# Gated attention and state-space mix on one core: parameters transposed by the DMA, maxima read from PSUM, dummy products, and a reordered prologue

## Chip, cores and metric

The kernel runs on one core of a Trainium2 chip. The metric is the time of one execution in microseconds (us), measured on the device. Three executions of the kernel before took 514.63, 514.94 and 518.87 us; the median is 514.94. A further execution, recorded by the hardware profiler, took 513.35 us. All durations below come from that recording.

The engines are named as in the profile: PE (TensorE, the matrix engine; PEld is its loading of weights), DVE (VectorE), ACT (ScalarE), POOL (GpSimd) and SP (SyncE, which here only issues DMA transfers). SBUF is the core's working memory and PSUM the memory into which PE writes.

## The reference

The input x has 2048 tokens of 448 channels (bfloat16). Two branches are computed from it and mixed by a gate:

- `g = sigmoid(sum(x * gate_w))`, one number per token.
- Branch a is attention with 16 query heads of width 28 that share one key head and one value head: `softmax(q k^T / sqrt(28)) v`, then a product with `wo`.
- Branch b is a long convolution of every channel along the tokens. Its kernel is generated from parameters: `K[d, l] = Re(sum_n C[d,n] * exp(l * dt[d] * A[d,n]) * dt[d] * B[d,n])`, with 256 complex terms per channel and 2048 positions. `u * Dskip` is added. A, B and C come as real and imaginary arrays of 448 x 256: six arrays, named A_im, A_re, B_re, B_im, C_re and C_im below, in the order in which the kernel numbers them (0 to 5).
- The result is `g * a + (1 - g) * b`.

## The kernel before

Attention is split into 1024 score tiles of 128 keys by 512 queries. Sets of three and two tiles alternate, 410 sets in all. For each set PE writes the scores to PSUM (`qk`, L1172 or L1181), ACT turns them into exponentials in SBUF (L1204), and PE multiplies these with the values (`pv`, L1218). The scores have two forms. The row-packed one (L1172) uses the 29 rows of one head; the full one (L1181) uses 128 rows and a copy of the queries, `qM`, in which other heads are zero. `qM` is filled by a DMA that POOL issues (L138). A set uses the row-packed form for sets 0 to 5, and from set 44 to 410 where it has three tiles.

Meanwhile DVE builds the powers of exp(dt A) for blocks of channels (`masters`, L845 to L865, and `tables`, L883 to L929; `BLOCKS` says which channels form a block), PE turns them into the convolution kernel (`kgen`, L949), which goes through DRAM (KP_scratch) and comes back as Toeplitz tiles `T`, and PE convolves (L1010). The input of the convolution, `U`, is x in another order: DMA loads put x into `O` (queue slots u0 and u1, eight transfers each), POOL copies it to `U` (L565, four copies for each half), and a DMA named du moves one half across partitions. The gaps of `U` are zeroed by four memsets beforehand (`consts`, on DVE before the change).

The order of the work is made by a planner (`Prog.schedule`) when the program is built. Every operation has an engine, a planned duration, a priority and lists of what it reads and writes. The planner runs a model of the engines and writes one list of instructions for each, in which the engine then works strictly in order; waits are put in where data or buffers require them. `pg.after[i] = j` tells the planner to place operation i after j and puts no wait into the program. Some constants steer the model: HEAD (how much later an operation may be ready and still be preferred for its longer path to the first exponential), FETCH, AHEAD, PORT. `tail` is the longest path from an operation to the first exponential, the planner's `goal`.

The prologue is the stretch up to that first exponential, and a short one behind it:

- SP issues the loads in one queue, in this order: the four quarters of x with wk and A_im between them, wq, wv, the other five parameters, zeros for Wo (zW), Dskip, the store xs1, a pad, xs2 and xs3, then u, wo and more. xs1 to xs3 store the transposed x of three quarters of the tokens to DRAM, from where they are read again later. The buffer of the last quarter is overwritten by the exponentials of the third set.
- PE transposes x (L606); ACT and DVE copy it out of PSUM (L615, L617); PE projects the keys (L620), with the key weight that L532 has copied into its padded form `Wk`. The keys stay in PSUM until ACT writes them to `kT` (L629).
- The largest absolute key of each quarter is needed for a bound on the scores that takes the place of the softmax's running maximum. DVE takes it from `kT` for the first three quarters (L633) and from PSUM for the fourth (L626).
- The maxima scale a mask into the weight `Wb` (L653, L654). For the first group of heads the queries are projected (L808), their maximum is taken (L814), the product with `Wb` is added (L817) and the result is cast to `qT` (L820). Then the first scores (L1172) and the first exponential can run. L534 and L536 copy the query weights to padded form.
- Each parameter arrives as 112 partitions by 1024 elements and is transposed by eight PE products into PSUM (`trans`, L738). DVE multiplies it (L749) with dt or with an earlier product. Between these, POOL reduces the angle (L752, L753) and makes the cosine term from a sine (L773, L774), and ACT computes sines, decays and squares (L758, L766, L769).
- The gate: ACT's exponential (L667), DVE's L669 to L671, a PE product (L686), a DVE copy `acc`, a second PE product (L696) and a copy to `omq` (L701).

## Time and profile before

| | us |
|---|---|
| runs | 514.63, 514.94, 518.87 (median 514.94) |
| the profiled execution | 513.35 |
| its span, first to last instruction | 511.6 |
| first exponential starts | 23.24 |
| last exponential ends | 500.97 |
| ACT busy | 485.7 |
| of that the 410 exponentials | 467.2 |

A group line of the profile names the source line, the engine, the operation and its tiles, then the count, busy time, mean ns of one, the idle time of the engine ahead of them and what ended it. A line of a timeline gives the start, the duration, the engine, source line, operation, tiles and count; several instructions that follow each other are one line; brackets hold the idle time before it and what released it. A line of the waits gives total us, count and longest. The rows of the page cut into 40 slices hold tenths: PEclk is the clock granted to PE. A row of a windows table names the stretch, its length, then for PE, PEld, DVE, ACT and POOL the busy time with the count of instructions, then the granted clock, the busy share of the DMA engines and GB/s.

Loads reach SBUF in the order of SP's queue. From the trace: the quarters of x land at 4.01, 6.72, 8.76 and 10.91, wk at 4.19, A_im at 7.68, wq at 12.29, A_re at 13.23, B_re, B_im, C_re and C_im at 14.06, 14.89, 15.98 and 16.95, zW at 18.25, the stores xs1, xs2 and xs3 at 19.39, 21.53 and 22.63, and u's first half at 25.75 us.

### The profile page before, as it was taken

What the parts mean: (1) busy time and instruction counts of PE and PEld (TensorE: products, weight loads), DVE (VectorE), ACT (ScalarE), POOL (GpSimd) and SP (SyncE); (2) the same over time, 40 slices, a digit from 0 to 9 for tenths busy, and PEclk for the clock granted to TensorE, in tenths of its full rate; (3) what the DMA queues carried; (4) which work ended last, traced back from release to release, by engine and by line L of the source; (5) the groups of instructions that cost most, each with busy time, mean ns of one, the idle gap of its engine ahead of it and who ended that gap; (6) DMA issues with size and microseconds to landing.
All of it is one profiled execution on the core that took longest, in us unless ns stands there. A gap on an engine that the chain in (4) does not pass through costs nothing.

```text
span 511.6 us, 18576 instructions
## 1 busy us (share of the span) xinstructions
PE 431.2 (84%) x8249; PEld 196.9 (38%) x8355; DVE 455.5 (89%) x823; ACT 485.7 (95%) x436; POOL 169.3 (33%) x297
## 2 busy tenths in 40 slices
PE   6679777788888899888887898998888888999895
PEld 5433113243333333443433443443443434444452
DVE  6888999999999999999999999999999999712434
ACT  5789999999999999999999999999999999999991
POOL 7541503451132151424243334305234343341000
PEclk9859999799999999999999999999999999999999
DMA  8912496799979889799989899899997998999992
GB/s 237 288 27 70 36 60 169 209 310 339 346 220 279 284 250 369 245 305 312 368 275 342 305 305 349 254 352 351 328 363 257 366 351 259 372 279 369 361 359 49
DMA packets 113425, 140.27 MB, mean 274 GB/s; under 512 B 45497, under 2 KB 52058, under 8 KB 113346
## 3 DMA queue, kind: packets, MB, share of 16 engines
q1 hardware_dynamic: 103600, 129.77, 79.3%
q0 software_dynamic: 8704, 9.25, 6.9%
q8 instruction: 65, 1.06, 0.9%
q10 hardware_dynamic: 1042, 0.07, 0.1%
q14 instruction: 14, 0.11, 0.1%
HBM read 128.39 MB, written 5.22 MB: 261 GB/s over the span
## 4 chain that ended last, share of the span: by engine, by line
DVE 56%; ACT 32%; PE 8%; issue 1%; POOL 0%; another core or an unknown queue 0%; POOLq 0%
ACT expT L1204 32%; DVE tab L902 8%; DVE tab L914 5%; DVE tab L913 5%; DVE tab L912 4%; DVE tab L911 4%; DVE tab L924 3%; DVE msq L845 3%; DVE tmp L920 3%; DVE mbf L865 2%; DVE seedz L849 2%; DVE seedz L847 2%; DVE cst L1020 2%; PE psS L1181 2%; DVE qT L814 1%
## 5 line engine op out<-in xcount | busy, mean ns | idle before, releaser
L1204 ACT ACTIVATE expT<-psS 128x1536 bf16<-128x1536 f32 (+1 forms) x410 | 467.2, 1352 | 8.1 <-PE psS L1172 5.5
L1181 PE MATMUL psS<-qM,kT 128*128 128x512 bf16 (+1 forms) x381 | 116.2, 374 | 33.5 <-ACT expT L1204 20.3
L1218 PE MATMUL psB<-expT,vaug 128*32 128x512 bf16 (+1 forms) x1088 | 103.5, 380 | 3.4 <-DVE acc L1079 2.8
L1172 PE MATMUL psS<-qT,kT 29*128 29x512 bf16 (+1 forms) x603 | 75.7, 377 | 26.4 <-ACT expT L1204 20.1
L138 POOL DMA_DIRECT2D KP_scratch<-kstg x112 | 61.4, 556 | 63.2 <-DVE kstg L964 41.5
L902 DVE TENSOR_TENSOR tab<-tab,mbf 128x512 bf16<-128x512 bf16 (+3 forms) x56 | 65.5, 1170 | 0.0
L1218 PEld LDWEIGHTS psB<-expT,vaug 128*32 128x32 bf16 x1088 | 26.8, 93 | 83.5 <-issue 76.9
L1181 PEld LDWEIGHTS psS<-qM,kT 128*128 128x128 bf16 x485 | 31.2, 98 | 61.7 <-ACT expT L1204 44.2
L138 POOL DMA_DIRECT2D rdenB<-R_scratch x56 | 28.9, 522 | 67.7 <-DMA R_scratch<-denT 48.7
L1010 PE MATMUL psS<-T,U 128*20 128x128 bf16 (+7 forms) x1792 | 45.3, 220 | 1.3 <-issue 0.9
L138 POOL DMA_DIRECT2D qM<-qT x64 | 33.1, 525 | 30.6 <-DVE qT L820 20.2
L914 DVE TENSOR_TENSOR tab<-tab 128x128 bf16<-128x128 bf16 (+4 forms) x70 | 42.7, 611 | 0.0
L913 DVE TENSOR_TENSOR tab<-tab 128x128 bf16<-128x128 bf16 (+4 forms) x70 | 41.9, 599 | 0.1
L1172 PEld LDWEIGHTS psS<-qT,kT 29*128 29x128 bf16 x603 | 18.7, 91 | 58.2 <-ACT expT L1204 45.0
L1010 PEld LDWEIGHTS psS<-T,U 128*18 128x18 bf16 (+7 forms) x1792 | 30.9, 94 | 18.6 <-issue 13.1
L138 POOL DMA_DIRECT2D R_scratch<-denT x14 | 8.9, 638 | 72.7 <-DVE denT L1071 40.2
L912 DVE TENSOR_TENSOR tab<-tab,mbf 128x4096 bf16<-128x4096 bf16 x14 | 32.0, 2288 | 0.1
L924 DVE TENSOR_TENSOR tab<-tab,tmp 128x4096 bf16<-128x4096 bf16 x14 | 32.0, 2284 | 0.1
L911 DVE TENSOR_TENSOR tab<-tab,mbf 128x4096 bf16<-128x4096 bf16 x14 | 32.0, 2287 | 0.0
L949 PE MATMUL psX<-tab 128*32 128x64 bf16 x1280 | 29.8, 242 | 0.3 <-DVE tab L929 0.2
L949 PEld LDWEIGHTS psX<-tab 128*32 128x32 bf16 x1280 | 23.8, 117 | 10.9 <-issue 6.5
L845 DVE TENSOR_TENSOR msq<-seedz 128x256 f32<-128x256 f32 (+2 forms) x50 | 26.3, 525 | 0.2
(165 smaller groups left out, 531.1 us busy)
## 6 DMA issues: line engine op xcount, KB each, us to landing
T<-KP_scratch SPq DMA_DIRECT2D x176, 512.0 KB, 8.5
U<-KP_scratch SPq DMA_DIRECT2D x48, 512.0 KB, 9.1
rdenB<-R_scratch POOLq DMA_DIRECT2D x56, 64.0 KB, 5.6
qM<-qT POOLq DMA_DIRECT2D x64, 32.0 KB, 5.3
tab<-in_A_x_dram SPq DMA_DIRECT2D x4, 448.0 KB, 5.6
O<-in_A_x_dram SPq DMA_DIRECT2D x16, 112.0 KB, 2.7
O<-cst SPq DMA_DIRECT2D x1, 1792.0 KB, 27.9
KP_scratch<-kstg POOLq DMA_DIRECT2D x112, 16.0 KB, 4.5
```

What stands on the lines that cost most here:

```text
L138: return [e.dma_start(o, i, **kw) for o, i in pairs]
L902: vo(lambda e, dst=dst, src=src, mri=mri: e.tensor_tensor(dst, src, mri, ALU.mult), 4 * n, done + mk(lv), [kr, ki, tk])
L911: vo(lambda e, src=src, mi=mi, tv=tv: e.tensor_tensor(tv, src, mi, ALU.mult), 2 * n, done + mk(lv), [tk])
L912: vo(lambda e, dst=dst, src=src, mr=mr: e.tensor_tensor(dst, src, mr, ALU.mult), 2 * n, done + mk(lv), [kr, ki, ("gap", s)])
L913: vo(lambda e, dc=dc, tc=tc: e.tensor_tensor(dc[0], dc[0], tc[1], ALU.subtract), n, [tk, kr], [kr])
L914: vo(lambda e, dc=dc, tc=tc: e.tensor_tensor(dc[1], dc[1], tc[0], ALU.add), n, [tk, ki], [ki])
L949: r = e.matmul(G.v(32 * g, 32, 256 * q + 64 * k, [[1, 64]]), tab.v(0, P, so, [[4, 32]]), tab.v(0, P, fo, [[mo - fo, 2], [4, 32]]), start=( ...
L1010: r = e.matmul(ps.v(32 * j, 32 - 2 * n, 128 * k, [[1, 128]]), self.U.v(0, P, (4 * gi + j) * 32 + 2 * n, [[1, 32 - 2 * n]]), tbuf.v(0, P, t ...
L1172: r = e.matmul(self.psS.v(0, P, 512 * b + o, [[1, n]]), kT.v(32 * h, DH + 1, 128 * kt, [[1, 128]]), qT.v(32 * h, DH + 1, 512 * (i % 2) + q ...
L1181: r = e.matmul(self.psS.v(0, P, 512 * b + o, [[1, n]]), kT.v(0, P, 128 * kt, [[1, 128]]), self.qM.v(0, P, (i % 2) * XQ + 512 * h + qo, [[1 ...
L1204: pg.op("act", lambda e: e.activation(expT.v(0, P, 512 * es[0], spread(es, n)), self.psS.v(0, P, 512 * bs[0], spread(bs, n)), AF.Exp, scal ...
L1218: r = e.matmul(self.psB.v(32 * h, 32, qo, [[1, n]]), vaug.v(0, P, 32 * kt, [[1, 32]]), expT.v(0, P, 512 * ring[t] + o, [[1, n]]), start=(k ...
```

## The change

- Five of the six parameters (`FLIP`, all but A_re) are loaded by a transposing DMA in the place of the plain load, in the layout that the products need. Their 40 PE products go; DVE's products read them from SBUF. A_re keeps its PE transposes.
- The maxima of all four key quarters are read from PSUM (L654 of the changed kernel), and ACT's copy of a quarter to `kT` waits for its maximum.
- PE gets 13 products of 128 x 512 whose result nobody reads: four ahead of the first transpose of x, nine behind the last key projection.
- The four memsets of U move from DVE to POOL, where they stand behind the reduction of the angle. `qM` is zeroed in eight pieces rather than two. The copy that pads `Wk` moves to POOL. POOL first runs one TENSOR_SCALAR and one TENSOR_TENSOR on a single element.
- POOL's product for the cosine term (L810 of the changed kernel) is placed behind the cast of the first queries, by planner order alone.
- Two intermediate products move from `O` to `mbf`, so that the second half of u no longer waits for them. As a result all eight copies to U stand in one row on POOL.
- The planner's choice before the first exponential is rewritten: among the operations whose start is not later than the earliest one's by more than HEAD (now 0.6) of its duration, it takes the one with the longest path to the goal. FETCH goes from 6200 to 5900, AHEAD from 3000 to 2000, and some durations and priorities change (kgen 1.3 to 1.45, yt 1.45 to 1.55, outp 1.75 to 1.65).
- BLOCKS goes from 2, 2, 3, 3, 4 to 2, 3, 3, 3, 3 chunks. Row-packed scores begin at set 24.
- The lists that follow: SP now issues the Dskip and wo loads behind all of u; on PE the gate's two products stand ahead of the scores of the fifth and the sixth set (before: later); on ACT the third exponential follows behind four of the five L769 operations (L805 of the changed kernel) where it followed behind one.

```diff
+FLIP = (0, 2, 3, 4, 5)
-BLOCKS = ((0, 2), (2, 2), (4, 3), (7, 3), (10, 4))
+BLOCKS = ((0, 2), (2, 3), (5, 3), (8, 3), (11, 3))
...
         def fn(e):
+            if flip:
+                return [e.dma_start_transpose(o, i) for o, i in pairs]
             return [e.dma_start(o, i, **kw) for o, i in pairs]
...
-                        if early is None or r < early[0][0] and (r + self.HEAD < early[0][0] or tail[i] >= early[1]) or r <= early[2] + self.HEAD and tail[i] > early[1]:
-                            early = ((r, o.pr, i), tail[i], min(r, early[2]) if early else r)
-                        early = (early[0], early[1], min(r, early[2]))
+                        early.append((r, o.pr, i))
                         continue
...
+                if early:
+                    key = min(early)
+                    while True:
+                        later = [k for k in early if tail[k[2]] > tail[key[2]] and k[0] <= key[0] + self.HEAD * ops[key[2]].ns]
+                        if not later:
+                            break
+                        key = max(later, key=lambda k: tail[k[2]])
+                    if best is None or key < best[0]:
+                        best = (key, e, key[2])
...
+        def warm(e, n, b):
+            t, o = self.bank(b)
+            for _ in range(n):
+                r = e.matmul(t.v(0, P, o, [[1, 512]]), V(self.ident, 0, P), self.ident.v(0, P, 0, [[0, 4], [1, P]]),
+                             start=True, stop=True, tile_position=(0, 0), skip_group_check=True)
+            return r
...
+        for _ in range(4):
+            self.warm(1, 3, 430)
+        tiny = V(sm, 14, 1)
+        pm(tiny, 0.0, 60, ["tiny"])
+        pg.op("pool", lambda e: e.tensor_scalar(tiny, tiny, MAGIC, -MAGIC, ALU.add, ALU.add), 60, rd=["tiny"], wr=["tiny"])
+        pg.op("pool", lambda e: e.tensor_tensor(tiny, tiny, tiny, ALU.subtract), 60, rd=["tiny"], wr=["tiny"])
...
-        for k in range(2):
-            pm(V(self.qM, k * XQ, XQ), 0.0, 1800, [("qM", k)], 1.5)
+        for k in range(8):
+            pm(V(self.qM, 512 * k, 512), 0.0, 470, [("qM", k // 4)], 1.5)
         for k in range(4):
-            dm(self.U.v(0, P, 16 + 3584 * k, [[32, 112], [1, 16]]), 0.0, 560, [("Uz", k)], 0.3)
+            pm(self.U.v(0, P, 16 + 3584 * k, [[32, 112], [1, 16]]), 0.0, 950, [("Uz", k)], 3.5)
...
         def lraw(k):
+            if k in FLIP:
+                pg.dma([(raw.v(0, P, k * 1024, [[D, 2], [1, D]]), dram(ins[names[k]], 0, [[NM, D], [1, NM]]))],
+                       (448, 512), f"raw{k}", wr=[("raw", k)], pr=0 if k < 2 else 0.2, flip=True, cost=1700)
+                return
...
-        pg.op("dve", lambda e: e.tensor_copy(self.Wk.v(0, DT, 0, [[32, 16], [1, DH]]),
-                                             wks.v(0, DT, 0, [[DH, 4], [0, 4], [1, DH]])), 300, rd=["wks"], wr=["Wk"])
+        pg.op("pool", lambda e: e.tensor_copy(self.Wk.v(0, DT, 0, [[32, 16], [1, DH]]),
+                                             wks.v(0, DT, 0, [[DH, 4], [0, 4], [1, DH]])), 640, rd=["wks"], wr=["Wk"])
...
-            self.late.append(pg.dma(lst, (1024, 896), f"u{k}", wr=[("ust", k)] + [("tp", 5), ("tp", 6)] * k, pr=0.3).i)
+            self.late.append(pg.dma(lst, (1024, 896), f"u{k}", wr=[("ust", k)], pr=0.3).i)
...
-            if q == 3:
+            if True:
                 pg.op("dve", lambda e, q=q, t4=t4, o4=o4: e.tensor_reduce(
                     sm.v(0, P, 8 + q, [[1, 1]]), t4.v(0, P, o4, [[1, 512]]), AX.X, ALU.max, apply_absolute_value=True), 600,
                     rd=[X], wr=[("km", q)])
...
-                rd=[X, "s0"] + [("km", 3)] * (q == 3), wr=[("kT", q)], pr=-2)
-            if q < 3:
+                rd=[X, "s0", ("km", q)], wr=[("kT", q)], pr=-2)
+            if False:
...
+        for k in range(9):
+            pg.after[len(pg.ops)] = self.k3
+            self.warm(1, 3, 225)
...
         def trans(k, pr):
+            if k in FLIP:
+                return raw.v(0, P, k * 1024, [[D, 2], [4, DT], [1, 4]]), ("raw", k)
...
+        pg.after[len(pg.ops)] = self.q0
         pg.op("pool", lambda e: e.tensor_tensor(t(4), t(4), t(4), ALU.mult), 1700, rd=[K(4)], wr=[K(4)], pr=0.3)
...
-            if s < 6 or 44 <= s < 411 and len(ts) == 3:
+            if s < 6 or 24 <= s < 411 and len(ts) == 3:
```

## The prediction

> **What bounds the kernel now.** The page's head and groups come first.
>
> ```profile
> PE 431.2 (84%) x8249; PEld 196.9 (38%) x8355; DVE 455.5 (89%) x823; ACT 485.7 (95%) x436; POOL 169.3 (33%) x297
> PEclk9859999799999999999999999999999999999999
> L1204 ACT ACTIVATE expT<-psS 128x1536 bf16<-128x1536 f32 (+1 forms) x410 | 467.2, 1352 | 8.1 <-PE psS L1172 5.5
> ```
>
> The span of 511.6 is ScalarE's: 467.2 us of softmax exponentials run almost back to back. In its timeline the first exponential starts at 23.24 and the last ends at 500.97; a tail of 10.6 follows. A change can win only before the first exponential, in the gaps between exponentials, or in the tail. ScalarE's waits are the second view:
>
> ```profile
> ACT expT L1204 <- PE psS L1172: 5.5, 8, 2.2
> ACT expT L1204 <- PE psS L1181: 2.5, 5, 0.8
> ```
>
> (Total, times, longest.) Of these 8.0, 2.16 is the wait before the first exponential; 5.8 are gaps. The ScalarE timeline places them, 2.35 by 50 us and the rest thin over the main loop:
>
> ```profile
> 23.24 1.45 ACT L1204 ACTIVATE expT<-psS 128x1536 bf16<-128x1536 f32 x1 [2.16 <-PE psS L1172]
> 32.48 1.45 ACT L1204 ACTIVATE expT<-psS 128x1536 bf16<-128x1536 f32 x1 [1.20 <-PE psS L1172]
> 34.36 1.02 ACT L1204 ACTIVATE expT<-psS 128x1024 bf16<-128x1024 f32 x1 [0.43 <-PE psS L1172]
> 49.38 1.45 ACT L1204 ACTIVATE expT<-psS 128x1536 bf16<-128x1536 f32 x1 [0.50 <-PE psS L1181]
> ```
>
> So everything here is worth single microseconds out of 515. The third view, VectorE's and GpSimd's timelines, shows what the first exponential waits for:
>
> ```profile
> 14.90 0.82 DVE L534 COPY Wq<-mbf 112x448 bf16<-112x448 bf16 x1
> 19.39 1.50 DVE L653 TENSOR_SCALAR Wb<-expT,small 128x128 bf16<-128x128 bf16 x1
> 20.93 0.35 DVE L654 SCALAR_TENSOR_TENSOR Wb<-expT,small,Wb 128x128 bf16<-128x128 bf16 x1
> 22.44 0.50 DVE L536 COPY Wq<-mbf 112x1344 bf16<-112x1344 bf16 x1
> ...
> 13.50 2.09 POOL L753 TENSOR_TENSOR T<-T 128x896 f32<-128x896 f32 x1
> 19.16 1.68 POOL L773 TENSOR_TENSOR T<-T 128x896 f32<-128x896 f32 x1 [3.57 <-ACT T L758]
> ```
>
> L653, on 128 elements, ends at 20.89, just after GpSimd's L773 (20.84). L534, a third of the size of L536, takes longer and ends at 15.72, just after L753 (15.59). L532 (5.44, 0.67 us for the same 448 elements) ends at 6.11, just after the second qM memset (2.30 + 3.67 = 5.97). I read all three as VectorE held until the GpSimd instruction ends, a memset included.
>
> **The change, part by part** (against the profiled execution: 513.35, its span 511.6; the median of the runs, 514.94, is 1.6 above it, and I carry the difference over). In the changed kernel's lines L563 is L536, L684 and L685 are L653 and L654, L717 and L731 are L686 and L696, L788 and L789 are L752 and L753, L810 is L773.
>
> *First exponential, gain.* L773 becomes L810 and is ordered behind the query cast, so it can no longer hold Wb. The last K projection leaves TensorE at 17.57 (17.19 + 0.38). Behind it in the new order come two K maxima from PSUM (0.60 apart, as L626 and L814 now), the query's maximum, two small steps (0.14, 0.14), L685 (0.35), TensorE (0.38), the query cast (0.69) and the lead from cast to exponential (23.24 - 22.53 = 0.71): 17.65 + 1.2 + 0.65 + 0.28 + 0.35 + 0.38 + 0.69 + 0.71 = 21.9, **-1.3**. The early maxima and VectorE's lost U memsets (1.89 to 5.52) bring no more: the projections wait for the landings of x (the fourth at 10.91).
>
> *U zeroed by GpSimd.* Four memsets of 1792 elements each; the qM memset of 2048 takes 1.84, so about 1.6 each and 6.4 together. In the new GpSimd order they follow L789 (before: ends 15.59), hence about 15.5 to 22: over the Wq copy L563 and Wb, both ahead of or in the chain above. Nothing is held at one end (0); at the other the copy waits a whole memset and Wb the rest of another, +2.5. L532 is the nearest row, and it was held: I take the copy's wait, **+1.5**.
>
> The Trainium skill, "SBUF — State Buffer", section "Who interferes with whom", makes the shared port pair an exclusive lock, but holds a VectorE operation with two SBUF inputs only against GpSimd operations that read SBUF. It names copies and tensor-with-scalar operations among those that take the pair; by it the memsets must hold L563 and Wb, and the end of nothing for this term falls away, rival 1 with it.
>
> *Dummy products and Wk copy.* Four 512-column products before any data, nine after the last K projection: 9 x 0.215 (spacing of L620 at 17 us) = 1.9, in a hole where PE idles 4.41 before L1172, so nothing; were Wb ready first they would cost up to 1.9. They may hold the clock: the window 21.60 to 38.50 has
>
> ```profile
> 21.60:38.50 16.90, 13.35 (x131) 6.59 (x133) 14.02 (x29) 13.63 (x15) 8.80 (x9) 0.50 0.27 74
> ```
>
> a granted clock of 0.50, and PE busy 13.35 of 16.90. The Wk copy now stands on GpSimd behind its first TENSOR_SCALAR; such a first one took 3.21 (L752) against 0.95 (L774). PE's tenth instruction waits for that copy, with all transposes of x behind it. Cover: the next x lands only at 6.72. Cost 0; without cover +2.
>
> *Transposes.* TensorE loses five groups of eight transposes, 0.93 each at half clock, 4.65 in all, four of them between 25.9 and 33.8. The gaps at 32.48 and 34.36 stand right behind such groups (PE itself waited 2.23 at 30.90 for VectorE to free a bank): **-1.6**. The gate's products move ahead of the fifth and sixth score sets, so the 0.50 at 49.38 goes: **-0.5**.
>
> *The same transposes as DMAs.* Unknown: no row has one. Plain, such a load of 224 KB lands 0.94 after the one before (14.06, 14.89, 15.98, 16.95). The nearest row by pieces is Wo<-cst (1024 pieces of 448 B, about 1.4 in its queue), giving 1.2 for 896 pieces; at the far end U<-U (28672 pieces of 32 B in 20.3) gives 81 us if every 2-byte element is a piece. I take 1.2. Behind them on SP stand zW, the pad, the stores of xT and u. The third of those stores lands at 22.63 now, and the third exponential, about 28, overwrites its source: free to 22.63 + 5 x (R - 0.94) = 28, so up to R = 2.1 per load; above that each us costs five. At 1.2: 0.
>
> The Trainium skill, "Advanced Engine Details and Errata", section "X-Bar Transpose (TRN2)", says that transposing DMAs are as fast as regular ones, 350 to 400 GB/s; by that a load takes some 0.6 (an estimate from that page), the term stays 0, and rival 3 has no chance. No row here shows it, so rival 3 keeps one.
>
> *The gate behind GpSimd's copies, a new wait.* u's second half no longer waits for the parameters, so all eight U copies run in one row from about 28 to 38 (before: four at 26.18 to 32.0, four at 52.67). L717 on PE now precedes the fifth score set, L731 the sixth; they wait for VectorE's sigmoid and its copy acc, which stand behind the three products of the parameters, the seeds and about fifteen short operations. Such operations are held one copy at a time:
>
> ```profile
> 26.18 5.82 POOL L565 COPY U<-O 128x896 bf16<-128x896 bf16 x4 [0.15 <-POOL T L774]
> ...
> 26.01 2.92 DVE L749 TENSOR_TENSOR seedz<-O,T 128x896 f32<-128x896 f32 x2
> 28.85 1.00 DVE L669 TENSOR_SCALAR gt<-gt 128x16 f32<-128x16 f32 x1
> ```
>
> L669, 16 elements, ends (29.85) with a copy (29.81). Two operations get through per copy, so ten of them take 5 x 1.15 = 5.8 where alone they take 2.9. VectorE reaches acc at about 35 to 37; the sixth set should start by 33. ScalarE's parameter work (five of 0.84) covers a part. Bounds 0 and +5; nearest row L669: **+1.5**.
>
> *Main loop and tail.* BLOCKS, priorities and row-packed scores from set 24 instead of 44 reorder VectorE and PE under the exponentials. A row-packed product takes 377 ns, a full one 374, and ScalarE hides both; 3.5 us of gaps remain there, so 0, bounds -1.5 and +1.5.
>
> **Sum**: -1.3 + 1.5 - 1.6 - 0.5 + 1.5 = -0.4, that is 512.95 for an execution like the profiled one, and **514.5** as median. 1% is 5.1 us, about what a measurement of this kernel can tell from no change.
>
> **Rivals.**
> 1. *Everything hidden, nothing held* (the memsets do not hold VectorE, copies and gate fit): -1.3 - 1.6 - 0.5 = -3.4: 511.5. For it: each hold is read from endings alone. Against: three rows end that way. 0.24.
> 2. *VectorE held throughout, slower*: from the memsets at full price (+2.5) and the gate at its upper bound (+5): -3.4 + 7.5 = +4.1, 519. For it: L653 and L669. It decides from the point where acc comes later than the sixth set's turn, about 33. 0.19.
> 3. *The DMA transposes are slow*: from R = 2.1 on, 5 us per us, with part returned because VectorE catches up meanwhile. The stores of xT and with them the third exponential stand at the end of SP's queue; R = 3.5 gives +7 less the gate's 1.5, 520; R = 5 about 527. For it: small pieces cost more in U<-U. Against: whole 512 B rows are read. 0.13, of which 0.08 above 520.
> 4. *The dummies hold the clock at full from 21.5 on*: the transposes' share of the gaps is gone anyhow, and the first score products run at 0.38 instead of 0.61: -0.5 more, inside the forecast.
>
> **How the numbers follow.** Forecast, within 2 us of 514.5: 0.44. The range takes in rival 1 with a better main loop (511.5 - 1) and rivals 2 and 3 up to R = 3.5: 510.5 to 520. Faster by over 1% (under 509.8) needs rival 1 and every main-loop gap together: 0.06. Slower by over 1% (over 520.1) is rival 3's upper part and rival 2 with a worse main loop: 0.13. Within: 0.81.
>
> **What would show it.** First exponential at 22 to 23.5, and L684 or L563 ending with a GpSimd memset (21.9 and short copies: rival 1). ScalarE without gaps after parameter transposes, but one of 1 to 3 ahead of the sixth set, "<-PE", with PE waiting for acc. Landings of the parameters 1.2 apart; over 2.1 apart and an exponential waiting for a DMA is rival 3. A new kind of gap in the main loop, or a tail other than 10.6, would be outside what I costed.

## The result

The changed kernel takes 521.78 us (median of 6, 518.88 to 526.28) against 514.85 for the kernel before: ratio 1.0146, 95% interval 1.0116 to 1.0177. It is slower. A second series gave 520.35 against 513.87, ratio 1.0105 (1.0055 to 1.0154). The forecast was 514.5, and the upper end of its range 520.0.

From the page of the changed kernel's first profile (span 524.5, the longest of the six executions, 526.28):

```profile
PE 454.1 (87%) x8328; PEld 196.9 (38%) x8328; DVE 457.5 (87%) x818; ACT 486.3 (93%) x436; POOL 177.4 (34%) x311
L1241 ACT ACTIVATE expT<-psS 128x1536 bf16<-128x1536 f32 (+1 forms) x410 | 467.5, 1358 | 20.0 <-PE psS L1209 12.6
```

The exponentials cost what they cost (467.5 after 467.2). ScalarE's idle time ahead of them went from 8.1 to 20.0: the loss is waiting, on TensorE's scores. The ScalarE timeline of the same profile places the first part of it:

```profile
24.03 1.45 ACT L1241 ACTIVATE expT<-psS 128x1536 bf16<-128x1536 f32 x1 [3.17 <-PE psS L1209]
36.41 1.45 ACT L1241 ACTIVATE expT<-psS 128x1536 bf16<-128x1536 f32 x1 [1.73 <-PE psS L1209]
40.20 1.02 ACT L1241 ACTIVATE expT<-psS 128x1024 bf16<-128x1024 f32 x1 [2.34 <-PE psS L727]
```

These are the gaps ahead of the fifth and the sixth set, 4.07 us where the prediction took 1.5. TensorE's timeline names what they wait for, the gate's products L717 and L727 (the second is the one that the prediction calls L731; the profile puts it at the line of its matmul):

```profile
35.16 0.61 PE L717 MATMUL psS<-onT,gt 128*16 128x128 f32 x2 [5.41 <-DVE gt L702]
38.16 1.32 PE L727 MATMUL psS<-acc,onT 16*128 16x64 f32 x5 [1.30 <-DVE acc L721]
```

And GpSimd's and VectorE's timelines tell why VectorE was late:

```profile
16.75 6.83 POOL L474 MEMSET U<- 128x1792 bf16 x4
23.97 1.68 POOL L810 TENSOR_TENSOR T<-T 128x896 f32<-128x896 f32 x1
27.83 1.29 POOL L811 TENSOR_SCALAR T<-T 128x896 f32<-128x896 f32 x1
29.26 10.63 POOL L592 COPY U<-O 128x896 bf16<-128x896 bf16 x8
...
17.14 1.61 DVE L563 COPY Wq<-mbf 112x1344 bf16<-112x1344 bf16 x1
20.65 1.32 DVE L684 TENSOR_SCALAR Wb<-expT,small 128x128 bf16<-128x128 bf16 x1
28.79 3.11 DVE L785 TENSOR_TENSOR seedz<-T 128x896 f32<-128x896 f32 x2
31.82 1.00 DVE L700 TENSOR_SCALAR gt<-gt 128x16 f32<-128x16 f32 x1
34.11 0.99 DVE L702 TENSOR_SCALAR gt<-gt 128x16 f32<-128x16 f32 x1
```

L563, 0.50 us before, takes 1.61, and Wb's first step 1.32 (1.50 before, where it ended with L773): both run inside the four memsets. On GpSimd L810 stands behind the memsets and L811 behind L810, so L811, which stood at 25.08 before (as L774), is at 27.83, and the copies to U follow right behind it. VectorE, held at several places on its way, reaches its two seed products at 28.79, when L811 is nearly done. The gate's three steps (L700 to L702) stand behind these products in VectorE's list, and by then the copies have begun: the products take 3.11 (2.08 in run b below, where no copy runs beside them), and L700 and L702, 16 elements each, take 1.00 and 0.99.

The second profile (span 517.4) shows that the two parts trade. Here VectorE came to L561, the copy that pads the first part of the query weights (L534 before), at 13.82, just before GpSimd began L789 (13.92), and it took 0.27; in the first profile VectorE came at 14.39, just behind (14.24), and it took 2.06. L563 then ran ahead of the memsets in 0.50, and the first exponential came at 22.13, nearly 2 us earlier. The gate was late all the same: VectorE now waited 2.23 us for L811, which the memsets hold back (ScalarE, then TensorE, GpSimd and VectorE):

```profile
22.13 1.45 ACT L1241 ACTIVATE expT<-psS 128x1536 bf16<-128x1536 f32 x1 [1.56 <-PE psS L1209]
35.08 1.45 ACT L1241 ACTIVATE expT<-psS 128x1536 bf16<-128x1536 f32 x1 [3.22 <-PE psS L1209]
38.87 1.02 ACT L1241 ACTIVATE expT<-psS 128x1024 bf16<-128x1024 f32 x1 [2.33 <-PE psS L727]
...
33.82 0.61 PE L717 MATMUL psS<-onT,gt 128*16 128x128 f32 x2 [7.12 <-DVE gt L702]
...
16.78 6.54 POOL L474 MEMSET U<- 128x1792 bf16 x4
28.49 0.95 POOL L811 TENSOR_SCALAR T<-T 128x896 f32<-128x896 f32 x1
29.57 10.07 POOL L592 COPY U<-O 128x896 bf16<-128x896 bf16 x8
...
29.47 1.09 DVE L785 TENSOR_TENSOR seedz<-T 128x896 f32<-128x896 f32 x1 [2.23 <-POOL T L811]
30.48 1.00 DVE L700 TENSOR_SCALAR gt<-gt 128x16 f32<-128x16 f32 x1
```

Gaps of 5.55 instead of 4.07. Of the 1.9 us of the early start 1.3 are left at the ninth exponential.

To split each run, the table compares the start of an exponential in its profile with the same one in the profile before: first the ninth (39.19 us before), then what is added from the ninth to the 406th. All against one execution of the kernel before (513.35, up to 1.5 us below its medians), and each profile is one execution too: that of c and the first of the changed kernel are the slowest of their series, that of h the fastest.

| run | ratio to before (95%) | ninth exponential | added to the 406th |
|---|---|---|---|
| changed kernel, first profile | 1.0146 (1.0116 to 1.0177) | +5.4 | +6.9 |
| the same, second profile | 1.0105 (1.0055 to 1.0154) | +4.0 | +1.8 |
| a: gate products behind set 10 | 1.0162 (1.0103 to 1.0221) | +2.3 | +6.5 |
| b: U memsets on VectorE | 0.9983 (0.9945 to 1.0020) | -0.7 | +1.3 |
| c: old main-loop constants | 1.0211 (1.0147 to 1.0275) | +5.3 | +9.8 |
| d: kernel before, new constants | 1.0026 (0.9996 to 1.0056) | +0.7 | +1.9 |
| e: copies to U behind the gate | 1.0113 (1.0076 to 1.0150) | +1.3 | +5.6 |
| f: kernel before, U memsets on GpSimd | 0.9961 (0.9941 to 0.9981) | -2.6 | +2.1 |
| g: no dummy products | 1.0082 (1.0045 to 1.0120) | +1.3 | +1.7 |
| h: b and e, L810 behind Wb | 1.0055 (1.0029 to 1.0082) | -2.3 | +3.5 |
| j: kernel before, DMA transposes | 1.0118 (1.0088 to 1.0147) | +0.9 | +5.7 |
| k: f and j | 1.0090 (1.0054 to 1.0126) | +3.6 | +1.1 |
| l: h, old main-loop constants | 1.0003 (0.9982 to 1.0024) | -0.9 | +0.8 |
| m: h, row-packed from set 44 | 1.0022 (0.9997 to 1.0047) | -0.6 | +2.3 |
| p: U memsets behind L811 | 0.9987 (0.9952 to 1.0023) | +1.7 | -0.6 |
| q: f, L773 behind Wb | 0.9982 (0.9955 to 1.0008) | -2.0 | +0.7 |
| s: j, gate products behind set 10 | 1.0012 (0.9984 to 1.0040) | -0.6 | +2.3 |

### The profile page after: what moved, and what is told of

It reads as the page before. It is cut to its first block, busy times and chain, and to the rows that moved or that the text cites. A ratio compares the mean times of both kernels' runs of the same rounds, so it can differ in the third digit from the quotient of the medians.

```text
span 524.5 us, 18635 instructions
## 1 busy us (share of the span) xinstructions
PE 454.1 (87%) x8328; PEld 196.9 (38%) x8328; DVE 457.5 (87%) x818; ACT 486.3 (93%) x436; POOL 177.4 (34%) x311
## 4 chain that ended last, share of the span: by engine, by line
ACT 43%; DVE 36%; PE 17%; issue 2%; DMA 1%; SPq 0%; DVEq 0%
ACT expT L1241 43%; DVE tab L939 5%; PE psS L1218 5%; PE psB L1255 3%; DVE tab L950 3%; DVE tab L951 2%; DVE msq L882 2%; PE psS L1209 2%; DVE tab L961 2%; DVE tab L949 2%; DVE tab L948 2%; PE psS L1047 2%; DVE mbf L902 2%; DVE tmp L957 1%; DVE seedz L886 1%
## 5 line engine op out<-in xcount | busy, mean ns | idle before, releaser
L1241 ACT ACTIVATE expT<-psS 128x1536 bf16<-128x1536 f32 (+1 forms) x410 | 467.5, 1358 | 20.0 <-PE psS L1209 12.6
L1218 PE MATMUL psS<-qM,kT 128*128 128x512 bf16 (+1 forms) x455 | 135.5, 386 | 15.3 <-ACT expT L1241 13.2
L1255 PE MATMUL psB<-expT,vaug 128*32 128x512 bf16 (+1 forms) x1088 | 106.2, 389 | 3.4 <-issue 1.8
L1209 PE MATMUL psS<-qT,kT 29*128 29x512 bf16 (+1 forms) x633 | 80.8, 382 | 24.0 <-ACT expT L1241 21.3
L1255 PEld LDWEIGHTS psB<-expT,vaug 128*32 128x32 bf16 x1088 | 27.0, 93 | 84.4 <-issue 79.5
L1218 PEld LDWEIGHTS psS<-qM,kT 128*128 128x128 bf16 x455 | 29.4, 98 | 57.5 <-ACT expT L1241 40.0
L1209 PEld LDWEIGHTS psS<-qT,kT 29*128 29x128 bf16 x633 | 19.8, 91 | 63.1 <-ACT expT L1241 48.8
L1047 PE MATMUL psS<-T,U 128*32 128x128 bf16 (+7 forms) x1408 | 36.7, 224 | 1.4 <-DVE O L1076 0.6
L1047 PE MATMUL psX<-T,U 128*32 128x128 bf16 (+7 forms) x1408 | 35.8, 224 | 0.9 <-DVE qT L857 0.7
L141 POOL DMA_DIRECT2D denT<-acc x14 | 10.0, 711 | 76.2 <-DVE acc L1116 69.9
L1047 PEld LDWEIGHTS psS<-T,U 128*32 128x32 bf16 (+7 forms) x1408 | 25.7, 96 | 17.0 <-issue 11.1
L1047 PEld LDWEIGHTS psX<-T,U 128*32 128x32 bf16 (+7 forms) x1408 | 25.0, 95 | 15.5 <-issue 9.9
```

The source lines that it names most:

```text
L141: return [e.dma_start(o, i, **kw) for o, i in pairs]
L1047: r = e.matmul(ps.v(32 * j, 32 - 2 * n, 128 * k, [[1, 128]]), self.U.v(0, P, (4 * gi + j) * 32 + 2 * n, [[1, 32 - 2 * n]]), tbuf.v(0, P, t ...
L1209: r = e.matmul(self.psS.v(0, P, 512 * b + o, [[1, n]]), kT.v(32 * h, DH + 1, 128 * kt, [[1, 128]]), qT.v(32 * h, DH + 1, 512 * (i % 2) + q ...
L1218: r = e.matmul(self.psS.v(0, P, 512 * b + o, [[1, n]]), kT.v(0, P, 128 * kt, [[1, 128]]), self.qM.v(0, P, (i % 2) * XQ + 512 * h + qo, [[1 ...
L1241: pg.op("act", lambda e: e.activation(expT.v(0, P, 512 * es[0], spread(es, n)), self.psS.v(0, P, 512 * bs[0], spread(bs, n)), AF.Exp, scal ...
L1255: r = e.matmul(self.psB.v(32 * h, 32, qo, [[1, n]]), vaug.v(0, P, 32 * kt, [[1, 32]]), expT.v(0, P, 512 * ring[t] + o, [[1, n]]), start=(k ...
```

## The experiments

**a. The gate's products later.**

```diff
+        self.g1 = len(pg.ops)          # first product of the gate
...
+            if s == 10:
+                pg.after[self.g1] = len(pg.ops)
```

> The changed kernel with the gate's first product placed behind the scores of set 10 by planner order. Theory (the gate's products on TensorE wait for VectorE, and the scores of the fifth and sixth set are queued behind them): ScalarE's gaps of 1.73 and 2.34 us before those sets go, the exponentials from the seventh set on start 3.5 to 4.1 us earlier than in the changed kernel, and the time falls from 521.8 to about 518. Rival (VectorE, held by the copies, is late for something else that the scores need as well): the gaps move to another of the first ten sets, and the time stays within 1 us of 521.8.

Both gaps went, and the ninth exponential came 3.0 us earlier than in the first profile of the changed kernel (+2.3 after +5.4), although the first one came at 24.84. So the scores do wait for the gate. The time did not fall, 522.55: a new gap of 5 us opened far behind, and it is systematic (four executions between 521.41 and 523.35). In ScalarE's and TensorE's timelines:

```profile
369.77 3.28 ACT L1244 ACTIVATE expT<-psS 128x1024 bf16<-128x1024 f32 x3 [5.04 <-PE psB L1258]
...
368.72 0.45 PE L1069 MATMUL psS<-ident,cst 128*64 128x64 bf16 x16 [1.98 <-DVE cst L1058]
369.32 0.83 PE L1258 MATMUL psB<-expT,vaug 128*32 128x512 bf16 x12 [0.15 <-DVE acc L1117]
```

TensorE stands at L1069, a step of the convolution, waiting for VectorE, with three groups of value products (x12) queued behind it, whose buffers the exponentials need. The order is the planner's, made anew by the edit. The same gap, at L1255 or L1232, is in e (4.97), h (4.65) and j (5.07), and in no other profile.

**b. U's memsets back on VectorE.**

```diff
-            pm(self.U.v(0, P, 16 + 3584 * k, [[32, 112], [1, 16]]), 0.0, 950, [("Uz", k)], 3.5)
+            dm(self.U.v(0, P, 16 + 3584 * k, [[32, 112], [1, 16]]), 0.0, 560, [("Uz", k)], 0.3)
```

> The changed kernel with the four memsets of U back on VectorE at the start. Theory (GpSimd's memsets hold VectorE's copies and Wb): the padding copies L563, L565 and L567 and Wb take under 0.6 us each where they took 1.3 to 1.6, the first exponential starts at about 22.3 instead of 24.0, the time falls by 1.5 to 2. Rival (VectorE's own 3.6 us of memsets delay the copies of the transposed x as much): first exponential at 23.2 to 24, the time stays within 1 us of 521.8.

The time fell by about 7 us, to 514.04, four times what was expected. The first exponential came at 22.67. The rest is the gate (GpSimd, then VectorE):

```profile
24.73 0.95 POOL L811 TENSOR_SCALAR T<-T 128x896 f32<-128x896 f32 x1
30.99 4.74 POOL L592 COPY U<-O 128x896 bf16<-128x896 bf16 x4 [5.32 <-DMA O<-in_A_x_dram]
...
29.08 0.16 DVE L700 TENSOR_SCALAR gt<-gt 128x16 f32<-128x16 f32 x1
29.84 0.16 DVE L702 TENSOR_SCALAR gt<-gt 128x16 f32<-128x16 f32 x1
```

L811 is 3.1 us earlier, the gate's steps take 0.16 each and end at 30.0, 5 us earlier, before the copies begin. But the new plan changed a second thing: SP issues the Dskip loads ahead of u here (at 16.10, in the changed kernel at 31.04), u's first half lands at 30.94 instead of 28.04, and the copies begin 1.7 us later than in the changed kernel. Had u landed at 28.04, L811 would have been done (25.68) and the copies would have met the gate's first step at 29.08; that is estimated from these times, no run shows it. So b does not price the memsets alone. Wb's step still takes 1.33: it now ends with L810 (18.88 + 1.68), which planner order alone does not keep behind it.

**c and d. The main-loop constants.** c puts the old blocks, priorities, FETCH, AHEAD, allowances and the form of sets 24 to 43 into the changed kernel; d puts the new ones into the kernel before.

```diff
-BLOCKS = ((0, 2), (2, 3), (5, 3), (8, 3), (11, 3))
+BLOCKS = ((0, 2), (2, 2), (4, 3), (7, 3), (10, 4))
...
-            if s < 6 or 24 <= s < 411 and len(ts) == 3:
+            if s < 6 or 44 <= s < 411 and len(ts) == 3:
```

> The changed kernel with the old blocks (2, 2, 3, 3, 4), row-packed scores from set 44, FETCH 6200, AHEAD 3000 and the old priorities and DMA allowances; prologue and its constants as changed. Theory (part of the loss is in the main loop, made by these constants): the late start of about 5 us at the eighth exponential stays, ScalarE's gaps behind 60 us fall from 10 to about 3.5, time about 518.5. Rival (the main loop's gaps follow from the shifted prologue or differ from run to run): gaps behind 60 us stay at 7 or more, time 521 to 522.

> The kernel before with only the main-loop constants of the change (blocks 2, 3, 3, 3, 3, row-packed scores from set 24, FETCH 5900, AHEAD 2000, priorities, DMA allowances). Theory (main-loop loss): first exponential at 23.2 as before, ScalarE's gaps behind 60 us 6 to 10 instead of 3.5, time 517 to 521. Rival (the loss sits in the prologue alone): within 1 us of the kernel before.

c fits neither: its start is as late (+5.3), and in its profile the main loop lost still more, with gaps of 2.0 to 2.1 us at 214 and 306. d lost 1.9 in the main loop and 0.26% in time, an interval that just reaches no change. The constants are not what makes the changed kernel slow; they may cost the 1 to 2 us that most of the table's new plans cost. One thing that they do move is the granted clock. By stage (the line from 68 to 112 us, with the clock in the third column from the end), the kernel before, d, and the changed kernel:

```profile
68.00:112.00 44.00, 35.44 (x531) 13.13 (x539) 43.23 (x87) 42.12 (x38) 15.87 (x29) 0.92 0.81 193
```

```profile
68.00:112.00 44.00, 37.83 (x506) 12.09 (x509) 42.11 (x71) 43.14 (x39) 15.21 (x29) 0.81 0.84 182
```

```profile
68.00:112.00 44.00, 36.82 (x471) 11.67 (x469) 41.64 (x69) 41.99 (x37) 13.65 (x25) 0.81 0.42 123
```

0.92 falls to 0.81 with the new constants, and c, with the old ones, has 0.92. ScalarE is busy 42 to 43 of the 44 us in all of them: the exponentials hide the slower products, so the lower clock is not where the time went.

**e. The copies behind the gate**, U's memsets still on GpSimd.

```diff
-                    rd=[("ust", k)], wr=[("U", k), ("ustd", k, j)] + uc, pr=1)
+                    rd=[("ust", k), "omq"], wr=[("U", k), ("ustd", k, j)] + uc, pr=1)
```

> The changed kernel, U's memsets still on GpSimd, with GpSimd's eight copies to U waiting for the gate's last VectorE copy omq. Theory (the gate is late because the copies hold VectorE's short operations one by one): first exponential at 24 as in the changed kernel, the sigmoid's end (L702) falls from 35.1 to about 31, the gaps of 1.73 and 2.34 us shrink to under 1 together, the eighth exponential starts 3 to 4 us earlier than in the changed kernel; time about 518 if the main loop keeps its gaps. Rival (the gate is late because the memsets have pushed the whole of GpSimd and VectorE back): L702 still ends after 33, gaps over 2.5 together.

The gate's operations are also planned earlier here (`prep_gate` ahead of `fill`), so that omq exists when the copies ask for it. In VectorE's timeline, then GpSimd's copy:

```profile
30.73 0.16 DVE L700 TENSOR_SCALAR gt<-gt 128x16 f32<-128x16 f32 x1
31.48 0.16 DVE L702 TENSOR_SCALAR gt<-gt 128x16 f32<-128x16 f32 x1
...
36.17 7.70 POOL L592 COPY U<-O 128x896 bf16<-128x896 bf16 x5 [7.31 <-DVE omq L732]
```

First exponential at 23.76, the memsets where they were (16.48 to 23.30), and the two gaps are gone; one of 0.58 is left ahead of the seventh set. The copies are what holds the gate, as expected. The ninth exponential came 4.1 us earlier than in the first profile. The time, 519.72, holds the 4.97 gap of the main loop.

**f. The memsets alone, in the kernel before.**

```diff
-            dm(self.U.v(0, P, 16 + 3584 * k, [[32, 112], [1, 16]]), 0.0, 560, [("Uz", k)], 0.3)
+            pm(self.U.v(0, P, 16 + 3584 * k, [[32, 112], [1, 16]]), 0.0, 950, [("Uz", k)], 3.5)
```

> The kernel before with only the four memsets of U moved to GpSimd. The planner puts three of them ahead of the reduction of the angle (L752) and one behind it. Theory (a memset on GpSimd holds VectorE's copies and delays GpSimd's own chain): VectorE is free from 1.9 to 5.5 but L752 starts at about 11.5 instead of 10.2, the angle chain is 1 to 3 us later, the first exponential comes at 23.5 to 25; the gate stands where it stood, so the loss stays at 0 to 2 us: 513.5 to 515.5. Rival (the memsets on GpSimd cost 7 us wherever they stand): about 520.

Better than the theory: 512.08 against 514.27, 0.4% faster than the kernel before (interval 0.2 to 0.6). The planner put three memsets at 6.05 to 10.95, ahead of the angle, and one behind it; Wb met none, nor L773, which came later:

```profile
6.05 4.90 POOL L464 MEMSET U<- 128x1792 bf16 x3
16.53 1.59 POOL L464 MEMSET U<- 128x1792 bf16 x1
21.23 1.68 POOL L773 TENSOR_TENSOR T<-T 128x896 f32<-128x896 f32 x1
...
18.64 0.30 DVE L653 TENSOR_SCALAR Wb<-expT,small 128x128 bf16<-128x128 bf16 x1
```

L653 falls from 1.50 to 0.30 and the first exponential comes at 21.21. Here too more than the memsets differs: x's last quarter landed 0.8 us earlier (10.15 after 10.91), and in this plan SP issues the Dskip loads later, so that u's first half lands at 31.78 instead of 25.75 and the copies no longer meet the gate. This is the fastest version that was run.

**g. Without the dummy products.**

```diff
-        for _ in range(4):
-            self.warm(1, 3, 430)
...
-        for k in range(9):
-            pg.after[len(pg.ops)] = self.k3
-            self.warm(1, 3, 225)
```

> The changed kernel without the 13 products whose result nobody reads. Theory (they stand in holes of TensorE and cost nothing): first exponential within 0.5 us of 24.0, time within 1.5 us of the changed kernel's 521.8; the clock may fall to 0.5 earlier than at 23.5. Rival (they held the clock up): the products of 512 columns before 23 us take 0.61 instead of 0.38 and the first exponential comes 1 us or more later.

518.68, some 2 to 3 us better than the changed kernel; neither theory as a whole. Of the rival, the clock came true: the granted clock falls to 0.50 at 19.1 us (at 24.4 and 26.9 with the dummies), and the first score products take 0.60, where they took 0.38 in the changed kernel. Yet the first exponential comes at 22.79. The plan differs: the memsets stand where they stood (16.80 to 23.35), but the gate's steps stand ahead of the seed product that waits for GpSimd, and the sigmoid ended at 27.9, ahead of the copies; only acc fell among them. The ninth exponential is at +1.3, and 3.5 us are lost in the tail (14.1 after 10.6). The run says that the dummies are not needed, not what they cost.

**h. Three holds taken away**: b's and e's edits, and

```diff
-        ... ALU.mult), 1700, rd=[K(4)], wr=[K(4)], pr=0.3)
+        ... ALU.mult), 1700, rd=[K(4), "kap"], wr=[K(4)], pr=0.3)
```

> The changed kernel with three edits: U's memsets on VectorE, the copies to U behind omq, and GpSimd's product L810 waiting for Wb (L685). Theory (each takes away one hold of VectorE): Wb's first step L684 takes 0.1 to 0.2 instead of 1.33, the first exponential starts at about 21.4 (22.67 with the memsets alone moved), the gate leaves no gap over 0.7, the eighth exponential starts about 1.5 us earlier than with the memsets alone moved: 512.5. Rival (the main loop absorbs it): within 1 us of 514.0.

The prologue did as expected: first exponential at 21.21, the ninth 2.3 us ahead of the kernel before. The time is 516.73, since the main loop's gap (4.65 at 363) took more than that back.

**j, k, s. The DMA transposes alone**, in the kernel before; with U's memsets on GpSimd; with the gate's products behind set 10.

```diff
+            if k in FLIP:
+                pg.dma([(raw.v(0, P, k * 1024, [[D, 2], [1, D]]), dram(ins[names[k]], 0, [[NM, D], [1, NM]]))],
+                       (448, 512), f"raw{k}", wr=[("raw", k)], pr=0, flip=True, cost=1700)
+                return
```

This is j; k adds f's line to it, s adds a's.

> The kernel before with only the five transposing loads (and without their 40 products on TensorE). Theory (the transposes' gaps go, and TensorE's freed places draw the gate's products forward in the plan): the gaps of 1.20 and 0.43 us behind the parameter transposes go, the first exponential stays at 22 to 23.5; the gate's second product now stands ahead of the sixth score set and waits there for acc, 0 to 4 us, depending on whether the four copies to U run at that time. 512.5 to 516. Rival (the transposing loads slow the loads behind them): the parameters land more than 2 us apart, the third exponential or u is late, 516 or more.

> The kernel before with the transposing loads and with U's memsets on GpSimd, where the planner puts three of them ahead of the angle's reduction. If the parts add up as in their own runs: the kernel before with the memsets alone is 0.4% faster, so this is 1.5 to 2.5 us under the same kernel with the transposing loads alone. If the memsets are harmful because the gate stands early (as in the changed kernel): slower than that kernel by 2 us or more.

> The kernel before with the transposing loads alone, and with the gate's first product placed behind the scores of set 10 by planner order. Theory (without transposes in TensorE's way the first exponentials run 1.6 us better, and the gate's early place takes it back): the eighth exponential starts 1.5 to 2.5 us earlier than in the kernel before, where it was 0.9 later with the gate early. If the stall of 5 us near set 290 belongs to a particular plan, it is gone or elsewhere here: 512 to 514; if it follows from the transposing loads, it stays: 518 or more.

j lost 1.2%: the gaps at 32.48 and 34.36 shrank to 0.47, the gate moved ahead of early sets and a gap of 2.19 stands at 37.37, and the new plan has the gap of 5.07 at 367. k has a gap of 4.71 at 35.81 (PE waited 4.3 for the gate's sigmoid and 3.2 for acc). GpSimd's copies in j, then in k:

```profile
30.92 7.75 POOL L574 COPY U<-O 128x896 bf16<-128x896 bf16 x4 [5.64 <-DMA O<-in_A_x_dram]
```

```profile
27.44 5.38 POOL L574 COPY U<-O 128x896 bf16<-128x896 bf16 x4 [1.16 <-DMA O<-in_A_x_dram]
```

VectorE begins the gate at the same time in both (27.25 and 27.33), so in k the memsets did not delay it. What differs is u: in k SP issues the Dskip loads behind u, u's first half lands at 27.39 (30.86 in j), the copies begin on top of the gate, and acc comes at 33.00 instead of 30.00. In s, with the gate late, the gaps of j are gone and the time is that of the kernel before (1.0012). So the loads are not at fault, but of the 1.6 us expected from the transposes' going nothing arrived between the first exponential (22.62 after 23.24) and the ninth (0.6 earlier, like the first): a gap of 1.35 at 36.23, behind five products of the next query projection that had moved into the room, took it.

**l and m. h with old constants.**

l is h with c's constants; m takes over only the form of the sets 24 to 43.

> The kernel with three edits (U's memsets on VectorE, copies behind omq, L810 behind Wb) and the old main-loop constants. Theory (the new constants cost about 2 us, and the plan made with them holds a stall of about 5 us near set 290): first exponential at 21.2, the eighth about 2 us ahead of the kernel before, no single gap over 2 us behind 60 us; 511 to 513. Rival (stalls of this size come with any new plan): gaps of 2 to 5 us elsewhere in the main loop, 515 or more.

> The same three edits with row-packed scores from set 44 again, the other constants as changed. Theory (the row-packed form occupies TensorE less and lets its clock fall between 60 and 90 us): granted clock 1.00 from 60 to 85 us, where it was 0.5 for 10 us; gaps between sets 24 and 60 fall by 0.5 to 1.5 us. Rival: the clock falls there all the same, no change in these gaps. In both the stall near set 290 may stay or move, since the plan is made anew.

l: no stall of 5 us, 514.27, no difference from the kernel before. The stall does not belong to the new constants, though: j has it with the old ones. m: neither has it, 516.04. Its granted clock from 50 to 112 us is 0.96 to 1.00, where h has 0.79 to 0.93, and yet the gaps from 55 to 115 us add up to 2.4 after 1.5 in h.

**o, p, q. What was still open.** o is the changed kernel once more (above). p orders the memsets behind L811:

```diff
+        for i in self.uz:              # the four memsets of U
+            pg.after[i] = len(pg.ops) - 1
```

> The changed kernel itself once more, for a second profile. If the split is 5 us in the prologue and about 2 in the main loop, the eighth exponential starts 4 to 6 us later than in the kernel before, and from there to the last one another 1 to 4 us are lost (the first profile lost 7, and was the slowest of six executions). If the main loop holds the larger part, that second number is 5 or more again. Time about 521.8.

> The changed kernel with U's memsets still on GpSimd, but placed behind the cosine's second step (L811) by planner order. Theory (what costs is that they stand between the angle and Wb): L563 and Wb are not held by a memset, the first exponential starts at about 22.5 instead of 24.0, the gate's sigmoid ends before the copies begin, the eighth exponential starts within 1.5 us of the kernel before; time 514 to 517. Rival (6.4 us of memsets on GpSimd cost wherever they stand): the eighth exponential 4 us or more late, as in the changed kernel, time 520 or more.

q is f with h's line, L773 behind Wb.

> The kernel before with U's memsets on GpSimd ahead of the angle's reduction, as in the run that was 0.4% faster, and with GpSimd's product L773 waiting for Wb. Theory (L773 holds Wb's first step): L653 takes 0.1 to 0.3 us, the first exponential starts up to 1 us earlier than in that run, time 511 to 512. Rival: L773, L774 and the seeds come later instead and the gain is lost within the first ten exponentials, or the new plan of the main loop loses it: 512 to 514.

p runs in 514.70, no different from the kernel before, with the same memsets, 6.6 us long, behind L811. Two more things moved in its plan: u's first half lands at 30.20 (Dskip ahead of u again), and the gate's second product stands behind the eighth set's scores, where a gap of 2.26 opens ahead of the ninth. It also shows which VectorE operations a memset holds (GpSimd, then VectorE; lines here are one or more above the changed kernel's, its L700 is L701):

```profile
25.80 6.58 POOL L474 MEMSET U<- 128x1792 bf16 x4
...
27.14 2.08 DVE L786 TENSOR_TENSOR seedz<-T 128x896 f32<-128x896 f32 x2
29.14 1.57 DVE L701 TENSOR_SCALAR gt<-gt 128x16 f32<-128x16 f32 x1
30.93 0.35 DVE L885 TENSOR_TENSOR msq<-seedz 128x256 f32<-128x256 f32 x1
```

The two-input products run at their usual 1.04 and 0.35 during the memsets; the tensor-with-scalar step takes 1.57 for 16 elements. During the copies, in the changed kernel, two-input products were held as well (the same 128 x 256 product took 1.08). The Trainium skill, "SBUF — State Buffer", section "Who interferes with whom", says just this, that two-input operations contend only with GpSimd operations that read SBUF; the trace agrees. Not each one is held, though: at 37.49 of the changed kernel's first profile, where it began within 0.01 us of a copy, the 128 x 256 product took 0.41.

q took 512.45 against 513.87. L653 took 0.29, but in its profile x was late (the last quarter at 11.69, in f 10.15) and the first exponential came at 22.84; the run does not tell q from f.

## Why the prediction was wrong

**What bounds the kernel** and where single microseconds can be lost held: the exponentials' own time did not change.

**First exponential, -1.3 and +1.5.** Forecast 23.4 (23.24 + 0.2); measured 24.03 and 22.13. The two parts were right in kind: L563 and L684 end with memsets. Whether L563 meets one depends on when VectorE gets there: in the second profile it ran just before them and only Wb was held (1.61). Not in the sum was L561, held for 1.8 us in the first profile behind L789.

**U zeroed by GpSimd, +1.5.** It asked what the memsets hold on VectorE, with +2.5 as the bound, and up to the first exponential that was about right. It did not follow GpSimd's own queue: behind the memsets stand L810 and L811, and through L811 VectorE's seed product and the gate. The gate's first step came at 31.82 and 30.48, in b at 29.08. That alone did not bring the gate among the copies: in g, with the memsets in the same place, the sigmoid was done before them.

**The gate behind the copies, +1.5: the step that failed.** The mechanism was as told, held operations one by one, L717 and the sixth set's scores waiting; the size was 4.07 and 5.55. The prediction looked for one gap, of 1 to 3 us, ahead of the sixth set, and that one came (2.34 and 2.33). For L717's wait ahead of the fifth set, which it names, it took no time of its own; there 1.73 and 3.22 were lost, because all steps of the sigmoid lay among the copies and it ended 3.8 to 5.1 us later than in b. Its working put acc at 35 to 37 for a turn at 33, that is 2 to 4 us, and let ScalarE's parameter work cover the rest; acc came at 37.83 and 36.50. Run e, which moves the copies away and leaves the memsets, takes both gaps off, 4.1 us at the ninth exponential. What brings the two together is the gate's late start and the early copies, and the runs do not separate these: in b and p, where the time came back, u also landed 2 to 3 us later, and in k early copies sufficed. A run with the memsets in place and only the Dskip loads ahead of u is missing. Rival 2 is what happened; its price, 519, is 1.4 to 2.8 us under the medians. The forecast added the two holds and did not see that one can make the other larger.

**Transposes, -1.6 and -0.5.** The gaps behind the transposes went in j and s, but other work moved into the room, and between the first and the ninth exponential s gained nothing. Cover removed from TensorE was not free room for the scores, because the planner fills it. Also not priced: the products now read two SBUF inputs and can be held. In the changed kernel two of them took 2.15 and 1.70 in the first profile (1.08 and 1.09 in the second) where L749 with one PSUM input took 1.08 and 1.02.

**The transposing loads, 0.** Right. In the first profile the parameters land at 7.6, 12.8, 13.5, 14.7 and 15.7, spaced 0.7 to 1.2 (1.2 was taken), the last 1.2 us earlier than before; in the second they are spaced 0.8 to 1.6, and the last lands at 17.2, 0.2 us later than before. Rival 3 did not occur. The Trainium skill, "Advanced Engine Details and Errata", section "X-Bar Transpose (TRN2)", has them as fast as regular loads, and with 0.8 to 1.1 between the plain ones before the trace agrees about.

**Dummies and Wk copy, 0.** The Wk copy cost nothing: 0.56 at 5.99, ahead of x's second landing. The clock stayed full until 24.4 and 26.9 (21.5 before, 19.1 in g without the dummies), and the first set's score products took 0.38 instead of 0.60, as rival 4 had it. Then it fell all the same, to 0.50 for 20.5 and 17.1 us (17.1 before); as rival 4 said, the effect is inside the forecast.

**Main loop, 0 with bounds of 1.5.** The other term that was too small. Measured +1.8 in the second profile and +6.9 in the first, which is that of the longest execution. In both about 3 us are lost at one place, between the 89th and the 109th exponential, while TensorE stands idle without a wait that the profile shows; first profile, then second:

```profile
153.95 0.50 PE L1255 MATMUL psB<-expT,vaug 128*32 128x512 bf16 x1 [1.81 <-issue]
```

```profile
152.11 0.39 PE L1255 MATMUL psB<-expT,vaug 128*32 128x512 bf16 x1 [1.86 <-issue]
```

There the granted clock falls to 0.50 for 3.4 us. The first profile has three more such stretches (at 233, 328 and 454 us), the second one (494), the kernel before none between 104 and 509. Why TensorE stops there is not known. Of 16 new plans 15 lost time between the ninth and the 406th exponential, ten of them 0.7 to 2.3 us, and four hold a gap of about 5 us. That the execution of before that serves as reference lies up to 1.5 us under its medians may make up part of the smaller losses. What decides whether a plan gets the 5 us gap was not settled; it comes with old constants (j) and new ones (a, e, h).

**Tail.** 10.4 and 10.6 from the last exponential's end to the span's, after 10.6: nothing there.

So of about 7 us some 4 to 5 lie in the prologue, most of it the gate among the copies, as e and a show by taking that away (4.1 and 3.0 us at the ninth exponential), and some 2 in the main loop; the second part is not traced to one edit. Nor did the end time follow in e and a, whose new plans hold the 5 us gap.

## What to carry to other kernels

When a step moves to another engine's queue, follow that queue first: what stands behind it there, who waits for that, and into whose way the delayed work then falls. Ask as well when that other work can start: whether the copies met the gate depended also on when u had landed. The version with the four memsets ahead of the chain was 0.4% faster, that with them in its middle 1.1 to 1.5% slower, and that with them behind it no different, but u's landing changed along with them. And in a kernel whose order a planner writes, an edit's own effect should be read at a fixed point near it (here the ninth exponential), because the new plan behind it moved the end as well, from -0.6 to +9.8 us here, nearly always up.

## What the runs showed beside that

GpSimd's first TENSOR_SCALAR of 896 elements still takes 3.2 us although the same operation ran on one element before (changed kernel, GpSimd's timeline):

```profile
2.04 0.23 POOL L500 TENSOR_SCALAR small<-small 128x1 f32<-128x1 f32 x1
...
10.93 3.23 POOL L788 TENSOR_SCALAR T<-T 128x896 f32<-128x896 f32 x1 [0.16 <-POOL onT L474]
```

So 3.2 us is not the price of being first, as I had read it. In all 18 profiles it is 3.21 to 3.23; the later one of the same shape, with other operators, takes 0.95 to 1.75.

A transposing load occupies SP's queue much longer than a plain one of the same size (SP's timeline, changed kernel):

```profile
6.13 0.43 SPq L141 DMA_DIRECT2D T<-in_B_A_re_dram  x1
6.60 1.35 SPq L140 DMA_TRANSPOSE T<-in_B_B_re_dram  x1
8.00 2.88 SPq L140 DMA_TRANSPOSE T<-in_B_B_im_dram  x1
```

0.43 against 1.29 to 2.88, 8.3 us for five. In this profile the parameters came no later for it, but u was issued at 18.62 instead of 17.07, and its first half landed at 28.04 instead of 25.75, still before the copies could begin.
